# Pair and single-tile pipeline of a two-layer expert kernel: when z banks are filled, which engine copies, where sums are kept, when small DMAs leave

## The chip, the cores and the metric

The kernel runs on one core of one Trainium2 chip. The metric is device time in microseconds of one execution; the time before is the median of three runs. Engines are called by the names that the profile uses: PE (TensorE, matmuls; PEld its weight loads), DVE (VectorE), ACT (ScalarE), POOL (GpSimd) and SP (SyncE, which issues the DMAs here).

## The reference

An attention-like recurrence (4 x 768 tokens, 8 heads of 40) gives x of 3072 rows by 320 columns. A soft mixture of experts follows: 32 slots are averages of all rows, run through 8 small networks, and each row mixes the 32 results back. The last layer, on which nearly all of the change lies, is:

```python
P = np.exp(logits - logits.max())          # logits = x @ w_gate, 3072 x 8
for _ in range(8):                         # Sinkhorn: rows, then columns
    P /= P.sum(1, keepdims=True) + 1e-09
    P /= P.sum(0, keepdims=True) + 1e-09
    P *= N / E
for e in range(E):                         # E = 8, w1: 320 x 1024, w2: 1024 x 320
    ye = np.maximum(x @ w1[e], 0.0) @ w2[e]
    out += P[:, e:e + 1] * ye
```

## The kernel before, in words

The first 190 us are the recurrence and the soft mixture; the change doesn't touch them. Since x has rank 32 after that mixture, `x @ w1[e]` is computed as a product over 96 rows: three stacked f16 parts of the 32 routed rows times w1 (tile `Sst[e]`, made by `s1_p`, `s1_h`, `s1_l`, or for later experts by `s1_v`, `s1_w`) with three parts of the mixing weights (`cst`). Values are kept as a pair of f16 numbers, a high part and a low remainder, so that a product is three f16 matmuls.

The 3072 rows are 24 tiles of 128. Expert 0 is done for the first 20 tiles in blocks of 512 columns (functions `g1`, `g2`; a step `st` is one tile of `g2` and two z banks of `g1`). Beside these steps a list `EXTRA` sets further work of the following expert, and `sinkhorn` runs at every odd step: nine small DVE instructions, with one matmul for the sum over partitions. `g2` ends with a copy of its result y from PSUM to `acc`.

After that the work is a list of units, written in slots. A slot is a group of matmuls of about equal length:
- `Old`: one of the last four tiles of expert 0, 4 slots.
- `One` (letter c): one tile, 4 slots of 6 matmuls of 320 columns; it needs two z banks.
- `Two` (letter P): two tiles i and j at once by a Strassen-like scheme (Winograd's form), 7 slots of 12 matmuls of 160 columns instead of eight; it needs four z banks. Its left operands are the two column halves of the two tiles and sums of them; its right operands are quarters of w2 and sums of them (`sum_w`, `sum_h`, `sum_l`).

Experts 1 to 6 have the pattern `cPPcP` three times (87 slots, 24 tiles), expert 7 the pattern `LAST`. A z bank is one PSUM bank of 512 columns, filled by four matmuls (`z_`, L1540); there are three of them (`psz`), and five other PSUM banks (`psu`) hold x, z and y of the units. `produce(k)` fills z bank number k of a unit 11 - k slots ahead of it, and plans what reads the bank: ACT takes the relu as a high part (`hi_z`, L1546), DVE takes the relu plus or minus another tile (`relu_with`, L1549). The f32 results stand in one tile `tmr` of five parts, called r22, r21, s1_, s2, s3, and s4 uses the place of s1_. From these ACT makes f16 high parts (`cast`, L1621) and POOL the low remainders (`lo_s`, L1552). The first sum s1_ is made by POOL (L1630), or by DVE for every third pair. The f16 operands of a pair stand in `opr[buf % 2]`, those of a single tile in `chl[buf % 3]`.

`consume(k)` issues slot k's matmuls (L1574 for single tiles, L1671 for pairs) and plans the drains: `keep_m`, `drain_x`, `drain_z`, a copy of m into the z bank of the unit, and `drain_y`, which adds the pieces into `acc` with the weights `Ps`.

What sets the order: PE, ACT, DVE and POOL take their instructions in the order in which the program writes them (`manual_schedule`), each engine by itself, held only by data; a slot number is a place in that order and no time. SP's order is left to the scheduler. `when[c]` holds the functions planned for slot c, in the order in which they were entered; functions entered with `early` come first.

Further work per expert e, planned by slots from its start c, serves expert n = e + 1 or n + 1: `load_w2` and `load_m2w` (weights from DRAM), `amax` (largest value of w2), `pow2_w` and `pow2_s` (a power of two as scale, of w2 and of the s1 weights), `prep_a`, `prep_x`, `prep_y` (scaled high and low part of w2), the `sum_*` functions, and `s1_p` to `s1_w`. The scale needs a maximum over partitions. `pow2` with `later` takes it by two DMAs: a column of 128 numbers to DRAM (`col`, L1111), and from there broadcast to all partitions (`row`, L1112); the first DMA leaves at the first of two planned slots (`spread`), and at the second one DVE reads `row` (`pow2_b`, L1124).

Of the kernel before, what the change touches and what calls it, by code (L numbers as in the profile page):

```python
# [20 lines left out]
def mlstm_moe_kernel(  # L21
# [1291 lines left out]
    def g2(n, tt, k0=0, k1=KF):  # L1313
        e, tb = divmod(n, NB)
        hh, hl = hs[n]
        ts = slice(tt * P, (tt + 1) * P)
        if k0 == 0:
            y0[tt] = psy.tile([P, TB], F32, tag="y", name="y")[:, 0:DM]
        y = y0[tt]
        for kc in range(k0, k1):  # L1320
# [16 lines left out]
        if e == E - 1:  # L1337
            nc.sync.dma_start(out=out[i * P:(i + 1) * P, :], in_=a)
# [152 lines left out]
    def b_(e, n, a):  # L1491
# [41 lines left out]
    tmr = op_a.tile([P, 5, KH, P], F32, name="tmr")  # L1533
# [20 lines left out]
    class One:  # L1554
        slots, banks, tiles = 4, 2, 1
# [53 lines left out]
    class Two(One):  # L1609
        slots, banks, tiles = 7, 4, 2  # L1610

        def __init__(self, e, i, j, buf):
            self.e, self.i, self.j, self.buf = e, i, j, buf

        def produce(self, k, at):
            o = opr[self.buf % 2]
            r22, r21, s1_, s2, s3 = (tmr[:, m] for m in range(5))
            s4 = s1_
            z = z_(self.e, self.j if k < 2 else self.i, (1, 0, 0, 1)[k])
            hi, lo = (lambda m: o[:, m, 0]), (lambda m: o[:, m, 1])  # L1620
            cast = lambda m, x: nc.scalar.copy(out=hi(m), in_=x)  # L1621
            if k == 0:
                at(0, lambda: hi_z(r22, z))
            elif k == 1:
# [6 lines left out]
                at(1, lambda: lo_s(lo(2), r22, hi(2)))  # L1631
            elif k == 2:
                at(0, lambda: hi_z(hi(0), z))
                at(0, lambda: relu_with(s3, z, r21, ALU.subtract))
                at(0, lambda: relu_with(lo(0), z, hi(0), ALU.subtract))
                at(1, lambda: cast(3, s1_))
                at(1, lambda: relu_with(s2, z, s1_, ALU.subtract))
                at(2, lambda: lo_s(lo(3), s1_, hi(3)))
                at(2, lambda: cast(4, s3))
                at(3, lambda: lo_s(lo(4), s3, hi(4)))  # L1640
            else:
                at(0, lambda: hi_z(hi(1), z))
                at(1, lambda: relu_with(lo(1), z, hi(1), ALU.subtract))
                at(2, lambda: relu_with(s4, z, s2, ALU.add))
                at(2, lambda: cast(5, s2))
                at(3, lambda: lo_s(lo(5), s2, hi(5)))
                at(3, lambda: cast(6, s4))
                at(4, lambda: lo_s(lo(6), s4, hi(6)))

        def consume(self, k, at):  # L1650
# [26 lines left out]
            if k == 2:  # L1677
                at(1, self.keep_m, True)
# [20 lines left out]
        def drain_y(self):  # L1699
# [3 lines left out]
            self.plus(self.i, self.z[:, DH:3 * DH].rearrange("p (a d) -> p a d", a=2))  # L1703
            self.plus(self.j, self.z[:, 0:DH].unsqueeze(1).to_broadcast([P, 2, DH]))
# [39 lines left out]
    def plan(c, f, *a):  # L1744
        when.setdefault(c, []).append(lambda: f(*a))
# [36 lines left out]
    def steps(c, fs):  # L1782
        for d, f in zip((0, 16), fs):
            plan(c + d, f)

    for e in range(1, E - 1):
        c = base + (e - 1) * PER
        n = e + 1
        if n + 1 < E:
            plan(c + 2, load_w2, n + 1)  # L1790
            plan(c + 36, load_m2w, n + 1)
            plan(c + 35, pow2_w, n + 1, lambda *f, c=c: steps(c + 35, f))
        for kk in range(4):
            if n + 1 < E:
                plan(c + (19, 20, 30, 31)[kk], amax, n + 1, kk)
            plan(c + (5, 6, 16, 17)[kk], prep_a, n, kk)
            plan(c + (7, 8, 18, 19)[kk], prep_x, n, kk)
            plan(c + (9, 10, 20, 21)[kk], prep_y, n, kk)
        plan_sums(c, n, (38, 39, 49, 50), (41, 42, 52, 53), (67, 68, 78, 79))
# [3 lines left out]
        for k in range(3):  # L1803
            plan(c + 54 + k, s1_w, n, k)
# [12 lines left out]
    for u, c in zip(units, starts):  # L1817
        if c == base:
# [50 lines left out]
```

## Time and profile before

| | us |
|---|---|
| median of three runs | 892.33 |
| all three | 887.03, 892.33, 1458.84 |
| profiled execution | 891.81 |
| its span | 889.9 |
| PE busy in the span | 860.4 (97%) |
| DVE busy | 705.0 (79%) |
| POOL busy | 629.2 (71%) |
| ACT busy | 593.3 (67%) |

The span goes from the first to the last instruction of the profiled execution; the 1.9 us to its own time lie around it. Matmuls are pipelined, so a busy PE is not PE at its peak. The granted clock was 0.994 of full over the span.

### The profile page before, as it was taken

What the parts mean: (1) busy time and instruction counts of PE and PEld (TensorE: products, weight loads), DVE (VectorE), ACT (ScalarE), POOL (GpSimd) and SP (SyncE); (2) the same over time, 40 slices, a digit from 0 to 9 for tenths busy, and PEclk for the clock granted to TensorE, in tenths of its full rate; (3) what the DMA queues carried; (4) which work ended last, traced back from release to release, by engine and by line L of the source; (5) the groups of instructions that cost most, each with busy time, mean ns of one, the idle gap of its engine ahead of it and who ended that gap; (6) DMA issues with size and microseconds to landing.
All of it is one profiled execution on the core that took longest, in us unless ns stands there. A gap on an engine that the chain in (4) does not pass through costs nothing.

```text
span 889.9 us, 27440 instructions
## 1 busy us (share of the span) xinstructions
PE 860.4 (97%) x11284; PEld 739.1 (83%) x11284; DVE 705.0 (79%) x1570; ACT 593.3 (67%) x1210; POOL 629.2 (71%) x632
## 2 busy tenths in 40 slices
PE   7999997899989998999999999999999999999998
PEld 5888884346667996999899989989999998998997
DVE  7777876456897786788988888888897977787886
ACT  7656653353365986787778677867787687676763
POOL 5766661000054886998898889889988988898883
PEclk9999999999999998999999999999999999999999
DMA  8999999960101031102120311041102000000111
GB/s 170 187 190 184 195 244 319 330 192 1 60 1 60 2 60 23 60 2 62 22 62 2 63 20 60 3 67 46 32 1 67 17 2 2 11 11 23 47 54 60
DMA packets 136117, 67.09 MB, mean 75 GB/s; under 512 B 105049, under 2 KB 129753, under 8 KB 135993
## 3 DMA queue, kind: packets, MB, share of 16 engines
q1 hardware_dynamic: 135721, 64.86, 30.2%
q8 instruction: 88, 1.44, 0.7%
q14 instruction: 36, 0.29, 0.2%
q10 hardware_dynamic: 224, 0.30, 0.1%
q0 software_dynamic: 48, 0.20, 0.1%
HBM read 60.10 MB, written 5.02 MB: 73 GB/s over the span
## 4 chain that ended last, share of the span: by engine, by line
PE 74%; DMA 11%; DVE 10%; ACT 3%; issue 2%; POOL 1%; SPq 0%; ACTq 0%; DVEq 0%
PE y L1574 14%; PE z L1540 7%; DMA bigy<-in_moe_w_dram 3%; PE pss L432 2%; DMA col<-mxs 2%; PE oa L477 2%; PE ptk L383 2%; DVE tmr L1549 2%; PE y L1321 2%; PE y L1322 2%; PE y L1323 2%; DMA wa<-in_moe_w_dram 1%; PE pe L402 1%; PE ob L488 1%; DVE op L1549 1%
## 5 line engine op out<-in xcount | busy, mean ns | idle before, releaser
L1552 POOL TENSOR_TENSOR op<-tmr,op 128x512 f16<-128x512 f32 x320 | 365.1, 1165 | 49.9 <-ACT op L1621 47.6
L1671 PEld LDWEIGHTS <-op 128*128 128x128 f16 x5376 | 376.6, 98 | 4.6 <-issue 2.9
L1621 ACT CAST op<-tmr 128x512 f16<-128x512 f32 x320 | 195.4, 617 | 43.3 <-DVE tmr L1549 37.0
L1549 DVE SCALAR_TENSOR_TENSOR tmr<-z,tmr 128x512 f32<-128x512 f32 x213 | 144.8, 682 | 52.5 <-ACT op L1546 39.4
L1574 PE MATMUL y<-wx,ch 128*128 128x320 f16 x960 | 152.9, 302 | 0.0
L1540 PE MATMUL z<-cst,sst 96*128 96x128 f16 x1344 | 131.4, 220 | 6.6 <-DVE tmr L1549 5.3
L1574 PEld LDWEIGHTS <-ch 128*128 128x128 f16 x960 | 89.4, 98 | 28.6
L1540 PEld LDWEIGHTS <-sst 96*128 96x128 f16 x1344 | 97.4, 98 | 17.9 <-DVE tmr L1549 8.4
L1546 ACT ACTIVATE tmr<-z 128x512 f32<-128x512 f32 x128 | 73.4, 594 | 37.3 <-PE z L1540 36.3
L1549 DVE SCALAR_TENSOR_TENSOR op<-z,op 128x512 f16<-128x512 f32 x128 | 86.9, 679 | 0.0
L1546 ACT ACTIVATE op<-z 128x512 f16<-128x512 f32 x128 | 77.1, 602 | 0.0
L1630 POOL TENSOR_TENSOR tmr<-tmr 128x512 f32<-128x512 f32 x43 | 54.7, 1272 | 28.8 <-ACT tmr L1546 24.1
L1549 DVE SCALAR_TENSOR_TENSOR ch<-z,ch 128x512 f16<-128x512 f32 x80 | 53.6, 683 | 6.7 <-ACT ch L1546 6.7
L1303 ACT ACTIVATE hh<-z 128x512 f16<-128x512 f32 x48 | 26.6, 595 | 35.4 <-PE z L1300 35.1
L1323 PE MATMUL y<-wh,hl 128*128 128x320 f16 x160 | 48.3, 302 | 0.3 <-DVE hl L1304 0.3
L1321 PE MATMUL y<-wh,hh 128*128 128x320 f16 x160 | 48.5, 303 | 0.0
L1322 PE MATMUL y<-wl,hh 128*128 128x320 f16 x160 | 48.4, 303 | 0.0
L411 ACT ACTIVATE dd<-pe 128x512 f32<-128x512 f32 x48 | 29.2, 609 | 28.7 <-PE pe L402 28.4
L1546 ACT ACTIVATE ch<-z 128x512 f16<-128x512 f32 x80 | 45.4, 592 | 4.2 <-PE z L1540 4.2
L1116 POOL PARTITION_ALL_REDUCE mr<-mx x3 | 1.1, 383 | 63.1 <-DVE mx L1091 37.9
L1475 POOL TENSOR_TENSOR raw<-raw 128x640 f32<-128x640 f32 x28 | 43.4, 1549 | 1.2
L1481 POOL TENSOR_TENSOR wt<-raw,wt 128x640 f16<-128x640 f32 x28 | 38.8, 1407 | 7.6 <-ACT wt L1478 7.6
(1188 smaller groups left out, 1752.4 us busy)
## 6 DMA issues: line engine op xcount, KB each, us to landing
wa<-in_moe_w_dram SPq DMA_DIRECT2D x18, 512.0 KB
raw<-in_moe_w_dram SPq DMA_DIRECT2D x28, 320.0 KB
kq<-in_k_dram SPq DMA_DIRECT2D x24, 160.0 KB
kq<-in_q_dram SPq DMA_DIRECT2D x24, 160.0 KB
vz<-in_v_dram SPq DMA_DIRECT2D x24, 160.0 KB
xr<-in_o_gate_dram SPq DMA_DIRECT2D x24, 160.0 KB
wb<-in_moe_w_dram SPq DMA_DIRECT2D x6, 640.0 KB
out_dram<-acc SPq DMA_DIRECT2D x24, 160.0 KB
```

The lines of the kernel that those rows point to most:

```text
L1321: nc.tensor.matmul(y, hh[:, kc, ts], wh[e][:, kc, :], start=(kc == 0), stop=False)
L1322: nc.tensor.matmul(y, hh[:, kc, ts], wl[e][:, kc, :], start=False, stop=False)
L1323: nc.tensor.matmul(y, hl[:, kc, ts], wh[e][:, kc, :], start=False, stop=(kc == KF - 1))
L1475: nc.gpsimd.tensor_tensor(out=quarter(e, *o), in0=quarter(e, *a), in1=quarter(e, *b), op=op)
L1540: nc.tensor.matmul(z[:, k, :], Sst[e][:, kc * P:(kc + 1) * P], cst[:, i * P:(i + 1) * P], start=True, stop=True,)
L1546: nc.scalar.activation(out=o, in_=z, func=AF.Relu)
L1549: nc.vector.scalar_tensor_tensor(out=o, in0=z, scalar=0.0, in1=x, op0=ALU.max, op1=op)
L1552: nc.gpsimd.tensor_tensor(out=o, in0=x, in1=h, op=ALU.subtract)
L1574: nc.tensor.matmul(self.y, self.at(a, kc), b[self.e][:, kc, :], start=(kc == a == 0 and b is wh), stop=(kc == KF - 1 and a == 1),)
L1621: cast = lambda m, x: nc.scalar.copy(out=hi(m), in_=x)
L1630: at(0, lambda: nc.gpsimd.tensor_tensor(out=s1_, in0=r21, in1=r22, op=ALU.add))
L1671: nc.tensor.matmul(t[:, c * DH:(c + 1) * DH], o[:, m, a, kp, :], b[kp], start=(kp == a == 0 and b is bh), stop=(kp == KH - 1 and a == 1),)
```

## The change

- Expert 0's copies from PSUM, on DVE for 16 of its tiles so far, go to ACT.
- `EXTRA` is regrouped: two `s1_c` at step 8 and two at step 10 instead of one at each of 9 to 12, and the weight sums are spread differently; two `sum_l` go into the slots 6 and 8.
- `tmr` gets a second home: a pair uses `tmr[buf % 2]`, and s4 takes the place of r22 instead of s1_. `chl` has two homes instead of three.
- A pair's z banks are filled 11, 10, 8 and 6 slots ahead (before: 11, 10, 9, 8), and some casts and remainders are planned one slot later.
- Each planned function has a rank, and within a slot the lowest rank runs first: readers of z banks 0, casts and the other copies beside them 1, drains 2, planned weight work 3.
- The copy of m into a unit's z bank comes before `drain_z`; `drain_y` is spread over four slots (`sum_y`, two `plus`, the rest).
- The weight maxima, the weight load and the trip of `pow2_w` come later in an expert (67 instead of 35, the load 62 instead of 36), the reader of a trip 18 slots after its start instead of 16, `s1_w` two slots later.
- Which pair takes its first sum on DVE is written in the pattern (D): in experts 1 to 6 the second of three, as before; in expert 7 none. Expert 7 has eleven pairs and two single tiles (before: ten and four).

```diff
-        if n == 0:
+        if e == 0:
             nc.scalar.copy(out=a, in_=y)
-            return
-        if e == 0:
-            nc.vector.tensor_copy(a, y)
             return
...
-             8: [(prep_a, 0), (prep_s, 0)], 9: [(prep_a, 1), (prep_s, 1), (s1_c, 0)],
-             10: [(prep_a, 2), (prep_s, 2), (s1_c, 1), (b_, 2, 1)], 11: [(prep_a, 3), (prep_s, 3), (s1_c, 2)],
-             12: [(sum_w, 0), (sum_w, 1), (s1_c, 3)], 13: [(sum_w, 2), (sum_w, 3)],
-             14: [(sum_h, 0), (sum_h, 1)], 15: [(sum_h, 2), (sum_h, 3), (sum_l, 0), (sum_l, 1)],
-             16: [(sum_l, 2), (sum_l, 3)]}
+             8: [(prep_a, 0), (prep_s, 0), (s1_c, 0), (s1_c, 1)], 9: [(prep_a, 1), (prep_s, 1)],
+             10: [(s1_c, 2), (s1_c, 3), (prep_a, 2), (prep_s, 2), (b_, 2, 1)], 11: [(prep_a, 3), (prep_s, 3)],
+             12: [(sum_w, 0), (sum_w, 1)], 13: [(sum_h, 0)], 14: [(sum_h, 1), (sum_w, 2), (sum_w, 3)],
+             15: [(sum_h, 2), (sum_h, 3)], 16: [(sum_l, 0), (sum_l, 1)]}
...
-    tmr = op_a.tile([P, 5, KH, P], F32, name="tmr")
+    tmr = [op_a.tile([P, 5, KH, P], F32, name="tm0")]
...
-        slots, banks, tiles = 7, 4, 2
+        slots, banks, tiles, at_z = 7, 4, 2, (0,1,3,5)
...
-            r22, r21, s1_, s2, s3 = (tmr[:, m] for m in range(5))
-            s4 = s1_
+            r22, r21, s1_, s2, s3 = (tmr[self.buf % 2][:, m] for m in range(5))
+            s4 = r22
...
-                if self.buf % 3 == 1:
-                    at(0, lambda: relu_with(s1_, z, r22, ALU.add))
+                if self.add_v:
+                    at(0, lambda: relu_with(s1_, z, r22, ALU.add), 0)
                 else:
-                    at(0, lambda: nc.gpsimd.tensor_tensor(out=s1_, in0=r21, in1=r22, op=ALU.add))
+                    at(0, lambda: nc.gpsimd.tensor_tensor(out=s1_, in0=r21, in1=r22, op=ALU.add), 1)
...
-                at(2, lambda: cast(4, s3))
-                at(3, lambda: lo_s(lo(4), s3, hi(4)))
+                at(3, lambda: cast(4, s3), 1)
+                at(4, lambda: lo_s(lo(4), s3, hi(4)), 1)
...
-                at(3, lambda: cast(6, s4))
-                at(4, lambda: lo_s(lo(6), s4, hi(6)))
+                at(4, lambda: cast(6, s4), 1)
+                at(5, lambda: lo_s(lo(6), s4, hi(6)), 1)
...
-                at(1, self.drain_z)
-                at(2, lambda: nc.scalar.copy(out=self.z[:, DH:2 * DH], in_=self.m))
+                at(1, lambda: nc.scalar.copy(out=self.z[:, DH:2 * DH], in_=self.m), 1)
+                at(2, self.drain_z)
             elif k == 6:
-                at(1, self.drain_y)
+                at(1, self.sum_y)
+                at(2, lambda: self.plus(self.i, self.z[:, DH:3 * DH].rearrange("p (a d) -> p a d", a=2)))
+                at(3, lambda: self.plus(self.j, self.z[:, 0:DH].unsqueeze(1).to_broadcast([P, 2, DH])))
+                at(4, self.drain_y)
...
-    LAST = "PPcPPPcPPPcPPc"
+    KINDS = {1: "cPDcP" * 3, E - 1: "PPPPPcPPPPPPc"}
...
-            zat.setdefault(max(c - LEAD[type(u)] + k, 0), []).append((u, k))
+            zat.setdefault(max(c - LEAD + u.at_z[k], 0), []).append((u, k))
...
-        when.setdefault(c, []).append(lambda: f(*a))
+        when.setdefault(c, []).append((3, lambda: f(*a)))
+
+    def run(c):
+        fs = when.get(c, [])
+        while fs:
+            fs.pop(min(range(len(fs)), key=lambda k: fs[k][0]))[1]()
...
-        for d, f in zip((0, 16), fs):
+        for d, f in zip((0, 18), fs):
             plan(c + d, f)
+    plan(6, sum_l, 1, 2)
+    plan(8, sum_l, 1, 3)
+    PLANS = {
+        1: ((5, 6, 16, 17), (7, 8, 18, 19), (9, 10, 20, 21), (38, 39, 49, 50), (41, 42, 52, 53), (67, 68, 78, 79),
+            (19, 37, 48, 66, 67)),
...
+        at_a, at_x, at_y, *at_s, at_m = PLANS[1]
         if n + 1 < E:
             plan(c + 2, load_w2, n + 1)
-            plan(c + 36, load_m2w, n + 1)
-            plan(c + 35, pow2_w, n + 1, lambda *f, c=c: steps(c + 35, f))
+            plan(c + 62, load_m2w, n + 1)
+            plan(c + at_m[4], pow2_w, n + 1, lambda *f, c=c + at_m[4]: steps(c, f))
...
-                plan(c + (19, 20, 30, 31)[kk], amax, n + 1, kk)
+                plan(c + at_m[kk], amax, n + 1, kk)
...
-            plan(c + 54 + k, s1_w, n, k)
+            plan(c + 56 + k, s1_w, n, k)
...
-            chl.append(ot.tile([P, 2, KF, P], F16, name="ch2", bufs=1))
+            tmr.append(ot.tile([P, 5, KH, P], F32, name="tm1", bufs=1))
```

## Rows read from the trace of the kernel before

**Rows 1.** Short stretches: us, PE, PEld, DVE, ACT, POOL busy (x instructions), PEclk, DMA.
```profile
600.00:700.00 100.00, 99.86 (x1320) 91.79 (x1318) 85.67 (x184) 75.57 (x151) 89.24 (x75) 1.00 0.12 36
260.00:265.00 5.00, 2.69 (x16) 1.71 (x15) 4.84 (x8) 2.06 (x4) 4.22 (x3) 0.86 0.00 0
265.00:270.00 5.00, 5.00 (x30) 3.16 (x29) 4.27 (x13) 0.73 (x2) 0.00 (x0) 0.79 0.00 0
350.00:355.00 5.00, 4.70 (x25) 2.86 (x24) 4.85 (x12) 3.98 (x9) 3.89 (x5) 0.50 0.19 59
800.00:805.00 5.00, 4.33 (x64) 4.00 (x62) 1.70 (x4) 2.33 (x6) 5.00 (x5) 1.00 0.01 3
810.00:815.00 5.00, 4.12 (x62) 3.99 (x61) 4.00 (x11) 3.08 (x8) 1.27 (x2) 1.00 0.00 0
```

**Rows 2.** The chain in order of time: start us, us, what.
```profile
298.66 0.83 PE mx__4507 L1671 x12
...
320.60 1.00 PE pu L1017 x16
...
412.29 1.00 PE pu L1017 x16
...
582.24 1.00 PE pu L1017 x16
...
666.91 1.00 PE pu L1017 x16
...
883.30 3.27 PE y L1574 x24
```

**Rows 3.** PE's own waits: total us, times, longest us.
```profile
PE z L1540 <- DVE tmr L1549: 5.3, 4, 4.1
...
PE z L1300 <- DVE hl L1304: 2.3, 1, 2.3
...
PE z L1540 <- DVE ch L1549: 0.9, 1, 0.9
```

**Rows 4.** Timeline, trips of experts 1 and 6: start us, us, engine, line, what.
```profile
323.95 0.33 SPq L1111 DMA_DIRECT2D col<-iv  x1
...
332.40 2.29 SPq L1111 DMA_DIRECT2D col<-mxs  x1
...
347.12 0.28 DVE L1124 TENSOR_REDUCE iv<-row 128x1 f32<-128x128 f32 x1 [6.81 <-DMA row<-col]
...
756.96 0.34 SPq L1111 DMA_DIRECT2D col<-mxs  x1
```

**Rows 5.** The tile row: reader's ns min/median/max, first and last start.
```profile
L1124 DVE TENSOR_REDUCE iv<-row x11: 273/276/286, 339.0 to 770.0; 128x1 f32<-128x128 f32 x11
```

**Rows 6.** Costliest groups 196 to 282 us (DVE), timeline 196 to 250 us (ACT).
```profile
L1332 DVE COPY acc<-y 128x320 f32<-128x320 f32 x16 | 7.8, 487 | 4.5 <-PE y L1323 4.1
...
201.82 1.13 ACT L1329 COPY acc<-y 128x320 f32<-128x320 f32 x3
```

**Rows 7.** Timeline of DVE and POOL, a Sinkhorn multiply and the weight sums.
```profile
256.56 1.56 DVE L1407 TENSOR_TENSOR Pm<-Pm,ca 128x192 f32<-128x192 f32 x1
...
266.70 0.36 DVE L1407 TENSOR_TENSOR Pm<-Pm,ca 128x192 f32<-128x192 f32 x1
...
257.87 6.51 POOL L1475 TENSOR_TENSOR raw<-raw 128x640 f32<-128x640 f32 x4
```

**Rows 8.** Waits from 788 to 890 us.
```profile
POOL op L1552 <- ACT op L1621: 6.3, 6, 1.8
POOL tmr L1630 <- ACT tmr L1546: 4.3, 2, 2.1
DVE tmr L1549 <- POOL op L1552: 4.0, 3, 2.5
```

**Rows 9.** The page's costliest groups, POOL's part of a pair.
```profile
L1552 POOL TENSOR_TENSOR op<-tmr,op 128x512 f16<-128x512 f32 x320 | 365.1, 1165 | 49.9 <-ACT op L1621 47.6
...
L1630 POOL TENSOR_TENSOR tmr<-tmr 128x512 f32<-128x512 f32 x43 | 54.7, 1272 | 28.8 <-ACT tmr L1546 24.1
```

More of the change, by code (lines that the diff above doesn't have):

```diff
@@ L1554, in mlstm_moe_kernel @@
     class One:
-        slots, banks, tiles = 4, 2, 1
+        slots, banks, tiles, at_z = 4, 2, 1, (0, 1)
         def __init__(self, e, i, buf):
@@ new lines, in produce @@
+                at(0, lambda: relu_with(s3, z, r21, ALU.subtract), 0)
+                at(0, lambda: relu_with(lo(0), z, hi(0), ALU.subtract), 0)
+                at(1, lambda: cast(3, s1_), 1)
+                at(1, lambda: relu_with(s2, z, s1_, ALU.subtract), 0)
+                at(2, lambda: lo_s(lo(3), s1_, hi(3)), 1)
+                at(3, lambda: cast(4, s3), 1)
+                at(4, lambda: lo_s(lo(4), s3, hi(4)), 1)
+            else:
+                at(0, lambda: hi_z(hi(1), z), 0)
+                at(1, lambda: relu_with(lo(1), z, hi(1), ALU.subtract), 0)
+                at(2, lambda: relu_with(s4, z, s2, ALU.add), 0)
+                at(2, lambda: cast(5, s2), 1)
+                at(3, lambda: lo_s(lo(5), s2, hi(5)), 1)
+                at(4, lambda: cast(6, s4), 1)
+                at(5, lambda: lo_s(lo(6), s4, hi(6)), 1)
@@ L1720, in mlstm_moe_kernel @@
         i = 0
-        for c in "cPPcP" * 3 if e < E - 1 else LAST:
+        for c in KINDS.get(e, "cPDcP" * 3):
             if c == "c":
@@ L1725, in mlstm_moe_kernel @@
             else:
-                units.append(Two(e, i, i + 1, twos))
+                units.append(Two(e, i, i + 1, twos, c == "D"))
                 twos += 1
             i += units[-1].tiles
-    PER = sum(u.slots for u in units if u.e == 1)
-    LEAD = {One: 11, Two: 11}
+    LEAD = 11
     starts, c = [], 0
@@ L1782, in steps @@
     def steps(c, fs):
-        for d, f in zip((0, 16), fs):
+        for d, f in zip((0, 18), fs):
             plan(c + d, f)
+    plan(6, sum_l, 1, 2)
[3 more added lines that the diff above has]
+            (19, 37, 48, 66, 67)),
+        2: ((8, 15, 22, 34), (14, 16, 33, 35), (16, 17, 34, 36), (37, 47, 58, 59), (41, 51, 66, 73),
+            (60, 76, 77, 78), (30, 34, 59, 61, 62)),
+    }
     for e in range(1, E - 1):
-        c = base + (e - 1) * PER
+        c = starts[next(k for k, u in enumerate(units) if u.e == e)]
         n = e + 1
+        at_a, at_x, at_y, *at_s, at_m = PLANS[1]
         if n + 1 < E:
             plan(c + 2, load_w2, n + 1)
-            plan(c + 36, load_m2w, n + 1)
-            plan(c + 35, pow2_w, n + 1, lambda *f, c=c: steps(c + 35, f))
+            plan(c + 62, load_m2w, n + 1)
+            plan(c + at_m[4], pow2_w, n + 1, lambda *f, c=c + at_m[4]: steps(c, f))
         for kk in range(4):
             if n + 1 < E:
-                plan(c + (19, 20, 30, 31)[kk], amax, n + 1, kk)
[L1796 to L1799, printed above, removed]
+                plan(c + at_m[kk], amax, n + 1, kk)
+            plan(c + at_a[kk], prep_a, n, kk)
+            plan(c + at_x[kk], prep_x, n, kk)
+            plan(c + at_y[kk], prep_y, n, kk)
+        plan_sums(c, n, *at_s)
         plan(c + 33, s1_p, n)
@@ L1821, in mlstm_moe_kernel, with at @@
             opr.append(ot.tile([P, 7, 2, KH, P], F16, name="op1", bufs=1))
-            chl.append(ot.tile([P, 2, KF, P], F16, name="ch2", bufs=1))
+            tmr.append(ot.tile([P, 5, KH, P], F32, name="tm1", bufs=1))
         for k in range(u.slots):
             s_ = c + k
-            def at(d, f, early=False):
-                fs = when.setdefault(s_ + d, [])
-                fs.insert(0 if early else len(fs), f)
+            def at(d, f, p=2):
+                when.setdefault(s_ + d, []).append((p, f))
             for v, kk in zat.pop(s_, ()):
                 if type(v) is One and kk == 0:
-                    v.h = chl[v.buf % 3]
+                    v.h = chl[v.buf % 2]
                 v.produce(kk, at)
             u.consume(k, at)
-            while when.get(s_):
-                when[s_].pop(0)()
+            run(s_)
     for c in sorted(when):
-        while when[c]:
-            when[c].pop(0)()
+        run(c)
     man4.__exit__(None, None, None)
```

35 lines of the change are left out of this document (12 added, 23 removed).

## The prediction

> **What bounds the kernel now.** I read the busy table by stretches first. Between 600 and 700 us TensorE (PE) shows 99.86 of 100 us busy, at full clock, with 1320 matmuls, while VectorE (DVE), ScalarE (ACT) and GpSimd (POOL) show 76 to 89 [rows 1]. Busy time of pipelined matmuls proves little, so the chain of waits in order of time came next: it shows where PE's own pace sets the time. Twelve matmuls of 160 columns take 0.83 us, 69 ns each; one has 160 columns, 66.7 ns at the 2.4 GHz level. Twenty-four of 320 columns take 3.27 us, 136 ns each [rows 2]. So in the repeated part PE runs within 4% of its floor. The routed-weight product that occurs once per expert starts at 320.60, 412.29, 582.24 and 666.91 us [rows 2]: 91.69 us for the first period, 169.95 for the next two, 84.67 for the last. One period is 87 slots, 63 of a pair (0.83 us) and 24 of a single tile (3.27/4 = 0.82 us), so 52.3 + 19.6 = 71.9 us, and 12.8 us are left for 48 z banks and that product. Nothing in a settled period is to be won by reordering, except what hides in those 12.8 us.
>
> The gain must therefore come from the places where PE isn't at its pace. PE's own waits from 200 us on name three [rows 3], and the short stretches show what each costs [rows 1]:
> A, 260 to 270 us, expert 0: one wait of 2.3 us for DVE, then a granted clock of 0.86 and 0.79 of full, a mixture of the two levels. 0.21 x 5 = 1.05 us, and a part of 0.14 x 5 = 0.7 us: 3.7 us together.
> B, 345 to 355 us, expert 1: one wait of 4.1 us for DVE, then 5 us at clock 0.50, which is the 1.2 GHz level. 91.69 - 84.67 = 7.0 us by the two periods.
> C, 800 to 815 us, start of expert 7: PE idles 5.00 - 4.33 and 5.00 - 4.12, 1.55 us.
> PE's other waits on tmr are 5.3 - 4.1 = 1.2 us [rows 3], up to 0.67 of it in C; of the 0.5 us left I count 0.4 as late trips in other experts. All this is 12.7 us, 1.4% of the profiled time of 891.81 us.
>
> **The change part by part.**
>
> *DMA trips apart (B).* The maximum over partitions travels to DRAM and back by two small DMAs, col and row, and DVE then reads row. In expert 1 the weight trip leaves at 323.95 and its reader runs at 339.0; only after its row has been issued does the s1 trip leave, at 332.40, and DVE waits 6.81 us at the head of its queue, to 347.12 [rows 4, 5]. Behind that waiting instruction stand the reads of the z banks, and PE waits for a bank. A trip by itself lasts 770.0 - 756.96 = 13.0 us in expert 6, and 15.1 us with a weight load beside it (323.95 to 339.0) [rows 4, 5]. The change moves the weight trip from slot 35 to 67 and the load from 36 to 62, so that the s1 trip at slot 37 goes alone; and it puts the reader 18 slots after the start instead of 16. A slot is about 84.67/87 = 0.97 us, so 17.5 us are there for 13.0 (s1) and 15.1 us (weights behind the load). Both fit, so B goes whole: 7.0 us; bounds 0 (SP's order keeps the s1 trip behind something else) and 7.0. The 0.4 us of other experts goes by the same step. The weight trip is now wanted at slot 85, its first use is at slot 5 of the next expert; the load at 62 is wanted at slot 33 of the next, some 55 us on. Writing the new s1 weights two slots later leaves 18 slots to the first z product that reads them. Those three cost nothing.
>
> *Expert 0's copies on ACT, and its extra work regrouped (A).* Sixteen DVE copies of 487 ns leave (7.8 us in all), and ACT takes them at 1.13/3 = 0.38 us [rows 6]. Two of the s1 conversions leave the steps in which PE waited. But DVE's lateness there has a second source: a Sinkhorn multiply on Pm takes 1.56 us at 256.56 and 0.36 us at 266.70, and in between POOL runs its weight sums without a gap from 257.87 for 6.51 us [rows 7]. Both operands of the slow one lie in SBUF; it ends just behind a POOL instruction. POOL's order hardly changes: it runs ahead of PE and is not held by slots. So I take DVE as about 0.5 us earlier by the copy and 0.5 us by the conversion in that step, 1.0 of the 2.3 us, and half a microsecond of slow clock: 1.5 us. Bounds: 3.7 us won, and 2.3 us lost, if ACT with its added copies becomes as late as DVE was.
> The Trainium skill, "SBUF — State Buffer", section "SBUF: two separate sides", says that a DVE instruction with two SBUF inputs and a GpSimd instruction exclude each other on a shared port pair, for the whole instruction. The stretched multiply agrees with it. It speaks against this part: as the POOL sums stay beside the Sinkhorn pass, the rule alone would leave A as it is, and the sum would be 1.5 us worse; that is a rival below.
>
> *z banks at slots 0, 1, 3, 5; z reads first; sums drained in steps; copy of m before the sum v.* No instruction is added or removed in a settled expert; PE issues the same matmuls in another place. PE's pace hides it, so 0. If that cover is gone, it shows as PE waits on a z bank: the f16 pieces of a pair are now finished up to 3 slots later (the last at slot -1 instead of -4, wanted at slot 6), so 7 slots, 6.8 us, remain for POOL to be late, and the sum on POOL must be there 3 slots after it is queued. Bounds: 48 z banks of 512 columns need 10.2 us at 2.4 GHz and the product at least its 1.00 us, so of the 12.8 us at most 1.6 can be gaps; I let half of that, 0.8 us in each of five experts, be winnable (4 us); on the other side stands a loss like C's 1.55 us at each of two groups of weight sums in six experts (18.6 us). I take 0, since the nearest rows, three periods at PE's pace with POOL at 89% [rows 1, 2], are of the same work.
>
> *f32 sums in two homes.* tmr double takes away the wait of DVE for POOL's reading of the first home, 4.0 us in three waits after 788 us [rows 8], which is what C hangs on. C goes: 1.5 us, bounds 0 and 1.55.
>
> *Eleven pairs in expert 7.* Two single tiles, 2 x 3.27 = 6.54 us, become one pair, 84 x 69 ns = 5.81 us: 0.7 us won. But now all eleven sums fall to POOL, none to DVE. POOL per pair: 5 x 1.165 + 1.272 = 7.10 us [rows 9]; PE per pair: 5.81 us and four z banks of 12.8/48 = 0.27 us, 6.9 us at most. In the runs of five and six pairs POOL falls back by at least 0.2 us a pair, and starts with two weight sums still to do, at 6.51/4 = 1.63 us no more than 3.3 us [rows 7]. For the expert POOL needs 11 x 7.10 + 3.3 = 81.4 us; PE needs 11 x 5.81 + 2 x 3.27 + 48 x 0.27 = 83.4 us for 85 slots. From the first sum (10 slots ahead) to the last piece (5 slots before the end) there are 90 slots, 88 us: 7 us of air. Before, POOL idled there 6.3 + 4.3 us for ACT [rows 8]. If all 10.6 us stay, PE waits 3.7 us; if none, 0. I take 1.4 us lost, somewhat under the middle, as the two homes remove some of what made ACT late. Bounds for the expert with C: 2.2 us won, 3.7 - 0.7 = 3.0 us lost. Taken: -0.7 - 1.5 + 1.4 = -0.8.
>
> *The sum*, against the profiled execution's 891.81 us: -7.0 - 0.4 - 1.5 + 0 - 0.8 = -9.7, so 882.1. The median shown is 892.33, 0.5 us above the profiled one; I say 882.
>
> **The rivals.**
> *All gaps close:* A goes whole and the z filling gives its 4 us. 882.1 - 2.2 - 1.4 (POOL keeps up) = 878.5, and with the 4 us 874.5. For it: C and A hang on DVE's order. Against it: settled periods repeat to 84.67 us.
> *POOL's sums stretch the Sinkhorn pass as before, so A stays, and POOL sets expert 7's pace:* 882.1 + 1.5 + 3.7 - 1.4 = 885.9, and 887.4 if C's wait comes back there too. For it: the stretched multiply, and 81.4 us of POOL work in an expert of 83.4 [rows 7, 9]. Against it: the 7 us of air.
> *The trips change nothing:* SP issues in another order than the slots, as expert 1's already differs from the later ones, and DVE waits on the s1 trip again. 882.1 + 7.4 = 889.5. Against it: 17.5 us of room for 13.0.
> *Slower: the sum on POOL is late in every expert.* Place: DVE's head waits in the third z bank's last read for POOL's sum, queued 3 slots before, when weight sums (1.63 us each) stand in POOL's queue; reads come before drains, so nothing passes. Price: C's 1.55 us for each of 12 groups, 18.6 us: 882.1 + 18.6 = 901. It decides from 9.7/12 = 0.8 us per group on. Against it: POOL is idle for 11% of a settled stretch [rows 1].
>
> **How the numbers follow.** Forecast (879 to 885): 0.48. All gaps close: 0.13. A and expert 7 (885 to 889): 0.19. Trips: 0.07. Slower: 0.13. About 2% is what a measurement of this kernel can tell from no change, 17.8 us: below 874.5 only if every gap closes and the clock helps, 0.04; above 910 only the far end of the slower rival, 0.05; within, 0.91. The range leaves out half of the slower rival and the tip of the best one: 875.5 to 894.
>
> **What would show it.** Right: the product of expert 1 and that of expert 2 stand 85 us apart; no DVE wait on row; PE's wait near 260 us shorter; in expert 7 no wait of DVE for POOL's pieces, but POOL busy over 95% there. Wrong: periods over 85.5 us in experts 2 to 6, PE waits on tmr that repeat by expert, DVE waits on POOL's sum.

## The result, and the profile after

The changed kernel takes 878.43 us against 891.27 us of the kernel before in the same job, a ratio of 0.9879 (95% interval 0.985 to 0.9907). Each median counts one slow run (1458.84 us before, 1114.23 us after), and the ratio leaves both out. The changed kernel is faster, clear of the noise and by less than 2%. The profiled execution took 878.75 us with a span of 877.0; the one before had a span of 889.9. The forecast was 882.0, with 875.5 to 894.0 as its range. The time lies in the range, 0.6 us under the band of 879 to 885 that had the largest chance.

The short stretches (columns as in [rows 1]) show PE at its pace in the places that were read there:

```profile
600.00:700.00 100.00, 100.00 (x1337) 92.99 (x1336) 86.41 (x185) 75.47 (x154) 90.46 (x78) 1.00 0.12 36
255.00:260.00 5.00, 3.81 (x25) 2.00 (x24) 2.92 (x11) 4.88 (x10) 2.27 (x3) 1.00 0.00 0
260.00:265.00 5.00, 4.16 (x31) 2.87 (x30) 4.86 (x8) 2.43 (x6) 4.84 (x4) 1.00 0.00 0
345.00:350.00 5.00, 5.00 (x61) 4.39 (x60) 4.35 (x10) 5.00 (x12) 4.23 (x4) 1.00 0.20 62
800.00:805.00 5.00, 5.00 (x77) 4.92 (x75) 4.02 (x11) 3.55 (x8) 5.00 (x5) 1.00 0.01 2
```

At 345 and 800 us the gaps B and C of [rows 1] are gone: PE is busy for 5.00 of 5.00 us at full clock. Near 260 us a gap remains: 3.81 and 4.16 us busy, with 25 and 31 matmuls, but the granted clock stays at 1.00, where it had fallen to 0.86 and 0.79 before. PE's own waits from 200 us on, which answer to [rows 3]:

```profile
PE y L1321 <- ACT hh L1303: 0.9, 1, 0.9
PE z L1300 <- DVE hl L1304: 0.8, 1, 0.8
PE y L1323 <- DVE hl L1304: 0.3, 1, 0.3
PE z L1536 <- DVE tm L1545: 0.2, 1, 0.2
```

The waits on tmr (now tm) are 0.2 us in all instead of 5.3. Those near 260 us are 0.9 + 0.8 + 0.3 = 2.0 us in three pieces, where there was one of 2.3. The starts of the routed-weight product, from PE's timeline, answer to [rows 2]; those not shown are 488.10, 572.43 and 656.75:

```profile
229.63 1.07 PE L1017 MATMUL pu<-wa,soT 128*32 128x256 f32 x16
...
319.10 1.07 PE L1017 MATMUL pu<-wa,soT 128*32 128x256 f32 x16
...
403.78 1.07 PE L1017 MATMUL pu<-wa,soT 128*32 128x256 f32 x16
...
741.08 1.07 PE L1017 MATMUL pu<-wa,soT 128*32 128x256 f32 x16
```

These starts cut the span into stretches whose lengths repeat between most runs to 0.1 us, much closer than whole times. In the table "to first" ends at the product for expert 1. "A" is from there to the product for expert 2; it holds the rest of expert 0 and the first 33 slots of expert 1. "p1" to "p5" are the periods of experts 1 to 5, each from slot 33 of the expert to slot 33 of the next (product to product). "last" is the rest of the span: 54 slots of expert 6, and expert 7. Each number is a difference of two starts in that run's trace, in us. There is one trace for each run, and e2 to e10 are one execution each.

| run | to first | A | p1 | p2 | p3 | p4 | p5 | last | span |
|---|---|---|---|---|---|---|---|---|---|
| before | 228.92 | 91.61 | 91.69 | 84.93 | 85.02 | 84.68 | 84.66 | 138.41 | 889.9 |
| after | 229.63 | 89.48 | 84.67 | 84.32 | 84.33 | 84.32 | 84.33 | 135.95 | 877.0 |
| e1 trips together | 228.68 | 89.48 | 89.42 | 90.36 | 90.29 | 88.74 | 91.05 | 135.89 | 903.9 |
| e2 weight trip at 35 | 227.70 | 89.48 | 87.24 | 85.35 | 85.12 | 84.78 | 85.09 | 135.94 | 880.7 |
| e3 reader at 16 | 227.59 | 89.48 | 84.33 | 84.32 | 84.33 | 84.32 | 84.33 | 135.88 | 874.6 |
| e4 banks 0 1 2 3 | 225.50 | 89.86 | 84.34 | 84.34 | 84.34 | 84.34 | 84.34 | 138.01 | 875.1 |
| e5 and one home | 227.48 | 89.95 | 84.98 | 84.71 | 84.70 | 84.91 | 84.71 | 139.70 | 881.1 |
| e6 expert 7 as before | 227.20 | 89.47 | 84.66 | 84.32 | 84.33 | 84.32 | 84.33 | 136.10 | 874.7 |
| e7 copies on DVE | 231.16 | 90.90 | 84.68 | 84.32 | 84.33 | 84.32 | 84.33 | 135.96 | 880.0 |
| e8 old list | 231.36 | 87.46 | 84.65 | 84.32 | 84.33 | 84.32 | 84.33 | 135.95 | 876.7 |
| e9 no ranks | 230.89 | 89.47 | 84.33 | 84.32 | 84.33 | 84.32 | 84.33 | 135.80 | 877.8 |
| e10 sums on DVE in expert 7 | 227.88 | 89.48 | 84.68 | 84.32 | 84.33 | 84.32 | 84.33 | 135.39 | 874.7 |
| e11 before, trips apart | 232.42 | 88.48 | 85.36 | 84.92 | 84.91 | 85.14 | 84.92 | 139.02 | 885.2 |
| e12 combined | 229.61 | 87.49 | 84.36 | 84.32 | 85.00 | 84.50 | 84.33 | 135.38 | 875.0 |

The stretch to the first product lies between 225.5 and 232.4 us. The only code in it that any run changes is the engine of some copies in its last part, and from ACT's first copy of y to the product all 14 traces have 27.10 or 27.11 us; the spread lies ahead of that, in code that is the same in all. It alone moves whole times by 7 us, so the stretches decide, not the spans. From before to after: A -2.13, p1 -7.02, p2 and p3 -1.30, p4 and p5 -0.69, last -2.46, to first +0.71; together -12.9.

### The profile page after: what moved, and what is told of

The parts are those of the page before. It is cut to its first block, busy times and chain, and to the rows that moved or that the text cites. A ratio compares the mean times of both kernels' runs of the same rounds, so it can differ in the third digit from the quotient of the medians.

```text
span 877.0 us, 27362 instructions
## 1 busy us (share of the span) xinstructions
PE 855.6 (98%) x11320; PEld 739.4 (84%) x11320; DVE 696.0 (79%) x1558; ACT 597.9 (68%) x1233; POOL 636.4 (73%) x641
## 4 chain that ended last, share of the span: by engine, by line
PE 86%; DMA 5%; DVE 5%; ACT 2%; SPq 1%; issue 1%; POOL 0%; ACTq 0%; POOLq 0%; DVEq 0%
PE y L1570 15%; PE z L1536 9%; PE pss L432 3%; DMA bigy<-in_moe_w_dram 2%; PE oa L477 2%; PE ptk L383 2%; DMA wa<-in_moe_w_dram 2%; PE y L1321 1%; PE y L1322 1%; PE y L1323 1%; PE pe L402 1%; PE ob L488 1%; DVE hl L1304 1%; PE pu L1017 1%; DMA wb<-in_moe_w_dram 1%; PE z L1300 1%
## 5 line engine op out<-in xcount | busy, mean ns | idle before, releaser
L1548 POOL TENSOR_TENSOR op<-tm,op 128x512 f16<-128x512 f32 x325 | 370.6, 1164 | 55.9 <-ACT op L1617 50.1
L1667 PEld LDWEIGHTS <-op 128*128 128x128 f16 x5460 | 382.9, 98 | 1.5
L1617 ACT CAST op<-tm 128x512 f16<-128x512 f32 x325 | 197.2, 616 | 23.3 <-POOL tm L1626 21.3
L1545 DVE SCALAR_TENSOR_TENSOR tm<-z,tm 128x512 f32<-128x512 f32 x213 | 145.8, 684 | 69.1 <-ACT op L1542 63.7
L1570 PE MATMUL y<-wx,ch 128*128 128x320 f16 x912 | 139.6, 299 | 0.0
L1542 ACT ACTIVATE tm<-z 128x512 f32<-128x512 f32 x130 | 76.6, 599 | 49.9 <-PE z L1536 40.1
L1570 PEld LDWEIGHTS <-ch 128*128 128x128 f16 x912 | 84.9, 98 | 27.9
L1626 POOL TENSOR_TENSOR tm<-tm 128x512 f32<-128x512 f32 x47 | 59.9, 1274 | 6.0 <-ACT tm L1542 6.0
L1451 POOL TENSOR_TENSOR wx<-raw,wx 128x640 f16<-128x640 f32 x28 | 39.2, 1402 | 10.4 <-ACT sst L1237 7.5
L1304 DVE SCALAR_TENSOR_TENSOR hl<-z,hh 128x512 f16<-128x512 f32 x48 | 31.1, 685 | 18.8 <-ACT hh L1303 18.8
```

Source lines behind the costliest of these rows:

```text
L1542: nc.scalar.activation(out=o, in_=z, func=AF.Relu)
L1545: nc.vector.scalar_tensor_tensor(out=o, in0=z, scalar=0.0, in1=x, op0=ALU.max, op1=op)
L1548: nc.gpsimd.tensor_tensor(out=o, in0=x, in1=h, op=ALU.subtract)
L1570: nc.tensor.matmul(self.y, self.at(a, kc), b[self.e][:, kc, :], start=(kc == a == 0 and b is wh), stop=(kc == KF - 1 and a == 1),)
L1667: nc.tensor.matmul(t[:, c * DH:(c + 1) * DH], o[:, m, a, kp, :], b[kp], start=(kp == a == 0 and b is bh), stop=(kp == KH - 1 and a == 1),)
```

## The experiments

**Trips: together again (e1).**

```diff
-plan(c + 62, load_m2w, n + 1)
+plan(c + 36, load_m2w, n + 1)
-for d, f in zip((0, 18), fs):
+for d, f in zip((0, 16), fs):
-plan(c + 56 + k, s1_w, n, k)
+plan(c + 54 + k, s1_w, n, k)
```

The weight trip goes back from slot 67 to 35 and the four maxima ahead of it from 19, 37, 48, 66 to 19, 20, 30, 31.

> The changed kernel with the four edits of the DMA trips undone: weight trip at slot 35, load at 36, reader 16 slots after the start, s1 writes at 54; all else as changed. Theory 1, the two trips of expert 1 stand one behind the other in SP's queue, and DVE waits for the second: the period from expert 1's product to expert 2's goes from 84.7 back to about 91.7 us, a DVE wait on row of about 6.8 us, the later experts lose 0.3 each, time about 886. Rival, the ranks and the other fill places took the sting out of it: DVE still waits on row but PE doesn't, period under 86, time under 880.

907.06 us, ratio to before 1.0209 (1.0162 to 1.0256). It is the largest effect of all, and it goes past both theories: each of the five periods is 89 to 91 us, not only expert 1's. SP's timeline in expert 1 of this run, and DVE's two reads behind it:

```profile
322.94 0.33 SPq L1111 DMA_DIRECT2D col<-iv  x1
...
331.23 0.32 SPq L1112 DMA_DIRECT2D row<-col  x1
331.64 0.38 SPq L1111 DMA_DIRECT2D col<-mxs  x1
339.87 0.32 SPq L1112 DMA_DIRECT2D row<-col  x1
...
339.02 0.28 DVE L1124 TENSOR_REDUCE iv<-row 128x1 f32<-128x128 f32 x1
...
344.75 0.28 DVE L1124 TENSOR_REDUCE iv<-row 128x1 f32<-128x128 f32 x1 [4.87 <-DMA row<-col]
```

Col of the weight trip, its row, only then col and row of the s1 trip: SP sits in the wait of row for col, and the second trip starts 8.7 us after the first. In the kernel before, only expert 1 had this order [rows 4]; from expert 2 on both cols left ahead of both rows, as in its SP timeline of expert 2:

```profile
415.34 0.33 SPq L1111 DMA_DIRECT2D col<-iv  x1
...
417.86 0.33 SPq L1111 DMA_DIRECT2D col<-mxs  x1
422.97 2.63 SPq L1112 DMA_DIRECT2D row<-col  x2
```

In e1 all five experts have the serial order. DVE's waits of this run (total us, times, longest), and PE in the five microseconds around the second read:

```profile
DVE iv L1124 <- DMA row<-col: 26.3, 5, 6.2
```

```profile
343.00:348.00 5.00, 1.71 (x20) 1.22 (x17) 3.15 (x10) 2.36 (x6) 1.20 (x2) 1.00 0.17 11
```

PE does 20 matmuls in 5 us, busy for 1.71. In the changed kernel SP's order hangs on where the trips are planned; how much of it is lost hangs on the reader as well, as the next run shows.

**Only the weight trip back (e2).**

```diff
-            (19, 37, 48, 66, 67)),
+            (19, 20, 30, 31, 35)),
```

> The changed kernel with the weight maxima and the weight trip alone back (slots 19, 20, 30, 31 and 35), the load planned at 62 and the reader at 18. Theory 1, the trips' places in SP's queue decide: a second trip that lands some 30 us after the first leaves has 2 slots (1.9 us) more than before, so DVE waits about 5 us on row and the period of expert 1 is 88 to 90 us. Rival 2, the place of the load or the two slots more decide: no wait on row, period 84.7.

Expert 1's period is 87.24, the later ones 0.5 to 1.0 us over the changed kernel's. SP issues in the same serial order as in e1, but DVE waits little:

```profile
DVE iv L1124 <- DMA row<-col: 2.7, 4, 1.0
```

```profile
344.26 0.28 DVE L1124 TENSOR_REDUCE iv<-row 128x1 f32<-128x128 f32 x1 [0.38 <-DMA row<-col]
```

2.7 us instead of 26.3, so both theories are half right. Most of the loss is gone (e1's sum of five periods is 449.9 us, e2's 427.6, the changed kernel's 422.0), and the distance between the trips takes the rest. Three edits lie between e1 and e2: the reader, the load and the s1 write. The load starts to leave SP 0.70 us behind the product in both. The reader is what the traces show: the second row is read at almost the same time (344.75 and 344.26), but in e1 DVE has only the four small instructions of the first trip between the two reads, while in e2 five reads and drains of z banks and units stand between them and run meanwhile. The s1 write was not moved by itself.

**Only the reader back (e3).** `zip((0, 18), fs)` becomes `zip((0, 16), fs)`.

> The changed kernel with the reader of a trip 16 instead of 18 slots after its start. Theory 1: a trip alone takes 12 to 13 us from col to landing, 16 slots are 15.5 us, so nothing changes: all periods 84.3 to 84.7, time 878 to 879. Rival 3, the two slots more are what takes the wait away: DVE waits 1 to 2 us on row in several experts, periods up to 86.

876.29 us, no DVE wait on row, and all periods 84.3. With the trips apart the two slots are worth nothing (expert 1's period is even 84.33 instead of 84.67); either edit alone takes away most of the loss.

**Trips apart on the kernel before (e11).** The edits of e1 in the other direction, on the kernel before.

> The kernel before with the trip edits alone (weight maxima at 19, 37, 48, 66, weight trip at 67, load at 62, reader at 18, s1 writes at 56). Theory 1: expert 1's period falls from 91.7 to 84.7, the next two from 85.0 to 84.7, the settled ones stay at 84.67; time about 884, 7 to 8 us under before. Rival: without the ranks the maxima and readers come at worse moments, and periods stay over 85; time 886 to 890.

885.47 us against 889.26, ratio 0.997 (0.9946 to 0.9995). The time gains 3.8 us, half of what theory 1 said. By the stretches expert 1's period falls by 6.33 us, but the other four rise by 0.60 together and the last stretch by 0.61. Moved alone, the planned work costs in other places: PE now waits for DVE on z banks of single tiles (ch), 2.6 us in six waits instead of the one of 0.9 in [rows 3]:

```profile
PE z L1540 <- DVE ch L1549: 2.6, 6, 0.9
```

A was not to change, as the code of expert 0's steps is that of the kernel before, yet it is 88.48 instead of 91.61. The whole difference lies in those steps: from the product to the last matmul of `g2` it is 40.66 us here and 43.79 before. In this run, POOL's four low parts of w2 (`prep_y`) and DVE's Sinkhorn instructions beside them answer to [rows 7]:

```profile
256.10 5.59 POOL L1454 TENSOR_TENSOR wx<-raw,wx 128x640 f16<-128x640 f32 x4 [7.05 <-ACT wx L1149]
260.06 0.37 DVE L1407 TENSOR_TENSOR Pm<-Pm,ca 128x192 f32<-128x192 f32 x1
260.85 0.87 DVE L1393 TENSOR_SCALAR rw<-rw 128x24 f32<-128x24 f32 x1
```

```profile
PE z L1300 <- DVE hl L1304: 0.8, 1, 0.8
```

POOL's line in the kernel before:

```profile
252.32 5.59 POOL L1454 TENSOR_TENSOR wx<-raw,wx 128x640 f16<-128x640 f32 x4 [6.77 <-ACT wx L1149]
```

The multiply starts 27.64 us after the product for expert 1 here (260.06 - 232.42) and before (256.56 - 228.92). POOL's four instructions start 23.68 us after it here and 23.40 before. So here the multiply begins just ahead of the fourth (256.10 and three times 1.39 make 260.27) and takes 0.37 us; before, it began just behind the start of the fourth (256.5) and took 1.56. PE then waits 0.8 us here, 2.3 before, where the clock fell. The wait of 1.5 us more and the 1.05 + 0.7 us of slow clock there [rows 1] make 3.25 us, against 3.13 of the stretch. So a shift of 0.28 us on POOL goes with 3.1 us. The shift is POOL's idle time ahead of the four, 7.05 us here and 6.77 before; what sets that isn't shown.

**The four banks (e4).**

```diff
-        slots, banks, tiles, at_z = 7, 4, 2, (0,1,3,5)
+        slots, banks, tiles, at_z = 7, 4, 2, (0,1,2,3)
...
-                at(5, lambda: lo_s(lo(6), s4, hi(6)), 1)
+                at(4, lambda: lo_s(lo(6), s4, hi(6)), 1)
```

The other casts and remainders that the change planned a slot later go back by one as well.

> The changed kernel with a pair's z banks filled at 11, 10, 9 and 8 slots ahead again, and the casts and remainders at the slots of before; two homes, ranks and the rest as changed. Theory 1, the places of z banks are worth nothing while PE sets the pace: periods 84.3 to 84.4, last stretch from expert 6's product to the end 135.9. Rival, the spread is where the 0.34 us per settled expert came from: periods 84.6 to 85, last stretch 136 to 138, and PE waits for z banks return.

Settled periods 84.34, unchanged; last stretch 138.01, 2.06 us more. Theory 1 holds for experts 1 to 6, the rival for expert 7, where up to six pairs follow each other. PE has one wait for DVE there, 0.6 us near 794 us, which the changed kernel hasn't; where the other 1.5 us arise isn't shown.

```profile
PE z L1536 <- DVE tm L1545: 0.6, 1, 0.6
```

**And one home (e5).** On e4: `tmr[self.buf % 2]` becomes `tmr[0]`, `s4 = r22` becomes `s4 = s1_`.

> As the run with banks at 11, 10, 9, 8, and one home of the f32 sums as well, s4 in the place of s1_. Theory 1, the second home is what removed the wait at the start of expert 7: the last stretch goes up by about 1.5 us against that run, with DVE waits for POOL's remainders of 3 to 5 us there; settled periods up by 0 to 0.3. Rival, the ranks removed it: last stretch unchanged within 0.3 us.

The last stretch rises by 1.69 to 139.70, settled periods by 0.36 to 84.70, about the kernel before's 84.67. DVE's waits for POOL's remainders between 400 and 700 us, and PE at the start of expert 7:

```profile
DVE tm L1545 <- POOL op L1548: 9.2, 10, 1.2
```

```profile
790.00:795.00 5.00, 3.52 (x53) 3.28 (x51) 1.85 (x5) 1.97 (x6) 5.00 (x5) 1.00 0.00 0
```

9.2 us of waits that the changed kernel and e4 don't have, and a gap of 1.48 us in PE as in C. The second home is what settled experts gained from.

**Expert 7 as before (e6), and its sums on DVE (e10).** The first added line is e6, the second e10.

```diff
-    KINDS = {1: "cPDcP" * 3, E - 1: "PPPPPcPPPPPPc"}
+    KINDS = {1: "cPDcP" * 3, E - 1: "PDcPPDcPPDcPPc"}
+    KINDS = {1: "cPDcP" * 3, E - 1: "PDPPDcPPDPPDc"}
```

> The changed kernel with expert 7 as before: ten pairs, four single tiles, the same three sums on DVE. Theory 1, the eleventh pair is worth its PE time alone: last stretch 135.95 + 0.7 = 136.7. Rival, POOL's eleven sums cost something that the new pattern pays: last stretch 135 to 136.

> The changed kernel with four of expert 7's eleven first sums on DVE instead of POOL. Theory 1, POOL at its limit costs PE nothing, since its lateness stays inside the 7 slots: last stretch 135.9 within 0.2, POOL 5 us less busy there. Rival, POOL sets expert 7's pace, as one of the forecast's terms had it (1.4 us): last stretch 134 to 135.

e6: 136.10, only 0.15 more than the changed kernel; the rival's range misses it by little, theory 1 by 0.6. e10: 135.39, 0.56 less, between theory 1 and the rival. The two fit together: the eleventh pair gains 0.7 us (136.10 to 135.39) when DVE helps, and POOL's eleven sums give 0.56 of that back. From 780 to 875 us, first in the changed kernel, then in e10 (POOL is the last busy time):

```profile
780.00:875.00 95.00, 93.64 (x1312) 90.04 (x1309) 80.14 (x172) 64.03 (x135) 84.03 (x74) 1.00 0.13 42
```

```profile
780.00:875.00 95.00, 91.37 (x1286) 88.34 (x1283) 80.81 (x173) 62.60 (x133) 77.73 (x68) 0.99 0.13 44
```

POOL falls from 84.03 to 77.73 us busy. Neither run has a PE wait in that stretch by the list of waits, so it isn't shown where the 0.56 us sit.

**Expert 0: copies back on DVE (e7), old list (e8).**

```diff
-        if e == 0:
+        if n == 0:
             nc.scalar.copy(out=a, in_=y)
             return
+        if e == 0:
+            nc.vector.tensor_copy(a, y)
+            return
```

> The changed kernel with expert 0's sixteen copies back on DVE, its extra work regrouped as in the change. Theory 1, DVE is the late engine beside the Sinkhorn pass: the stretch from expert 1's product (near 229 us) to expert 2's goes from 89.48 to 90.5 to 92. Rival, ACT with its added copies is the late one now, as PE's wait of 0.9 us on hh shows: the stretch falls to 88 to 89.

Stretch A 90.90, 1.42 us more: theory 1. In e8 `EXTRA` is that of the kernel before, and the two `sum_l` at slots 6 and 8 go back into it:

> The changed kernel with the list of expert 0's extra work as before (one s1 conversion at each of the steps 9 to 12, the weight sums at 12 and 13), copies on ACT. Theory 1, what is lost near 260 us hangs on how Sinkhorn's DVE instructions fall beside POOL's sums, and regrouping gains nothing sure: stretch 88 to 90, with other instructions stretched. Rival, the regrouping is what gained: stretch 90.5 to 91.6.

Stretch A 87.46, 2.02 us less than the changed kernel and under theory 1's 88 to 90. So the regrouping loses, and the copies win. PE's waits from 228 to 300 us, e7 and then e8:

```profile
PE y L1321 <- ACT hh L1303: 1.4, 1, 1.4
PE z L1300 <- DVE hl L1304: 1.2, 1, 1.2
PE y L1323 <- DVE hl L1304: 0.3, 1, 0.3
```

```profile
PE z L1300 <- DVE hl L1304: 0.5, 1, 0.5
```

In sum PE waits 2.9 us in e7, 2.0 in the changed kernel and 0.5 in e8, so that these waits hold 0.9 of e7's 1.42 us and 1.5 of e8's 2.02. How the new list loses is in ACT's, DVE's and POOL's timeline of the changed kernel:

```profile
250.93 0.18 DVE L1390 TENSOR_SCALAR rw<-rw 128x24 f32<-128x24 f32 x1
...
254.11 0.47 ACT L1229 ACTIVATE sst<-pu,sc 32x256 f16<-32x256 f32 x1 [1.34 <-DVE sst L1233]
...
253.60 0.48 DVE L1233 SCALAR_TENSOR_TENSOR sst<-pu,sc,sst 32x256 f16<-32x256 f32 x1
...
257.71 1.29 DVE L1304 SCALAR_TENSOR_TENSOR hl<-z,hh 128x512 f16<-128x512 f32 x2 [1.85 <-ACT hh L1303]
...
260.12 1.13 DVE L1390 TENSOR_SCALAR rw<-rw 128x24 f32<-128x24 f32 x1
...
259.82 1.40 POOL L1451 TENSOR_TENSOR wx<-raw,wx 128x640 f16<-128x640 f32 x1 [1.61 <-ACT raw L1447]
```

With two s1 conversions in one step, ACT waits 1.34 us for DVE's part of the first before it begins the second, its relus come later, and DVE idles 1.85 us for them before its Sinkhorn pass, which then meets POOL's work: a 128 x 24 instruction takes 1.13 us instead of the 0.18 at 250.93. In e8 the pass is met as well, but DVE hasn't waited for ACT before it:

```profile
256.79 1.29 DVE L1304 SCALAR_TENSOR_TENSOR hl<-z,hh 128x512 f16<-128x512 f32 x2
...
259.24 1.09 DVE L1390 TENSOR_SCALAR rw<-rw 128x24 f32<-128x24 f32 x1
```

**Ranks (e9).** `fs.pop(min(...))` becomes `fs.pop(0)`, first entered, first run.

> The changed kernel without ranks: within a slot functions run in the order in which they were entered, so planned weight work comes first, as before. Theory 1, with two homes and trips apart the ranks are worth little: settled periods 84.3 to 84.5, last stretch within 0.5 of 135.95. Rival, the ranks keep z reads from waiting behind weight work of 0.8 to 1.6 us: periods 84.7 to 86, PE waits on z banks, last stretch 137 or more.

Periods 84.3, last stretch 135.80: the ranks are worth nothing here, theory 1.

**Combined (e12).** The changed kernel with e8's list, e10's pattern and e3's reader.

> The changed kernel with three of its parts taken back: expert 0's extra work listed as before, four of expert 7's first sums on DVE, the reader 16 slots after a trip's start. Theory, the parts add up as the single runs showed them: the stretch from expert 1's product to expert 2's 87.5 us (-2.0), expert 1's period 84.33 (-0.34), settled periods 84.33, last stretch 135.4 (-0.55): 2.9 us under the changed kernel, 875.5 us, ratio to before 0.982 to 0.986. Rival, the gain near 260 us hangs on how instructions happen to fall and doesn't come again: stretch 89 to 90, time 877.5.

876.79 us, ratio to before 0.9839 (0.9811 to 0.9866). A is 87.49 and the last stretch 135.38, both as the single runs had them. With the reader at 16 slots, though, two periods are 85.00 and 84.50: so close, a trip is sometimes late, and DVE waits on row, 0.9 us of it in expert 3:

```profile
DVE iv L1124 <- DMA row<-col: 2.2, 5, 0.9
```

The interval overlaps the changed kernel's (0.985 to 0.9907); that this version is better is likely by the stretches (1.99 less in A, 0.57 in the last one) and not shown by the times.

## Why the prediction was right, and where its steps were not

**B** was forecast at 7.0 us and measured 7.02 in expert 1's period. The mechanism held: one trip behind another in SP's queue, DVE at the head of the wait. By the runs the trips are worth somewhat less, 6.33 us in e11, and some 0.36 us of the 7.02 belong to the second home (e5). One step was wrong: "the load from 36 to 62, so that the s1 trip at slot 37 goes alone". SP's order isn't bound to slots, and in the changed kernel the load still leaves right behind the product, 7 us ahead of the s1 trip, whose reader then runs without a wait:

```profile
319.80 2.03 SPq L677 DMA_DIRECT2D wa<-in_moe_w_dram  x4
326.91 0.33 SPq L1111 DMA_DIRECT2D col<-mxs  x1
334.31 0.33 SPq L1112 DMA_DIRECT2D row<-col  x1
...
358.06 0.41 SPq L1111 DMA_DIRECT2D col<-iv  x1
...
343.62 0.28 DVE L1124 TENSOR_REDUCE iv<-row 128x1 f32<-128x128 f32 x1
```

What went apart is the weight trip (358.06 instead of 323.95). The 13.0 and 15.1 us of a trip were read from col's issue to a reader that didn't wait, so they are upper bounds; a trip alone takes about 12 us (last section). The price of the order was also not a constant: 3.8 us by e11 on the kernel before, and 907.06 against 878.43 us in the changed one, where SP's order made all five experts serial. The late trips of other experts were forecast at 0.4; of the 1.30 us in p2 and p3, about 0.7 belongs to the second home by e5.

**A** was forecast at 1.5 us and measured 2.13, but by other terms. "0.5 us earlier by the copy and 0.5 us by the conversion": the copies are worth 1.42 in e7, and the regrouping costs 2.02 in e8. These two don't sum to -2.13. But e11, with expert 0's code of the kernel before, has 88.48, and from there they nearly close: 88.48 - 1.42 + 2.02 = 89.08, against 89.48, which seven runs with the changed kernel's code of expert 0 and banks give within 0.01; 0.4 us stay open. So the 2.13 us are measured against an unlucky meeting of DVE and POOL in the profiled execution of before; how often that kernel meets it is open. Measured from e11, the two edits of expert 0 lose 1.0 us together, so that the term came out near its size is luck. What was won against that execution is the clock: PE's waits near 260 us went from 2.3 to 2.0 us only, but the 1.75 us that the slow clock cost there [rows 1] are gone, of which the forecast had counted half a microsecond.

The forecast's second source, the Sinkhorn pass stretched beside POOL's work, is there in all runs read, and the pair of before and e11 shows that the moment of the meeting decides. By the rule of the Trainium skill, "SBUF — State Buffer", section "SBUF: two separate sides", of a DVE instruction with two SBUF inputs and a GpSimd instruction that reads SBUF, whichever starts first holds a shared port pair for the whole instruction, and the other one waits. The trace agrees: the multiply took 0.37 us when it began just ahead of POOL's instruction, and 1.56 just behind its start. The rival drawn from this rule, that A stays as long as the pass is stretched, doesn't follow: in e8 PE's wait is 0.5 us with the pass still stretched.

**Settled experts** were forecast at 0, with 0.8 us per expert as a bound for smoother z filling. They gained 0.34, and the term was put to the wrong edit: the spread of the banks gives nothing there (e4), the second home 0.36 (e5), which the forecast priced in expert 7 alone. PE's idle time doesn't show it: DVE's ten waits for POOL in e5, 0.9 us on average, leave no wait in PE's list. The kernel before with its trips apart (e11) has 84.91 to 85.14 us there and e5 84.70 to 84.91, so some 0.2 us more may belong to edits that no run took back alone: the drains, the copy of m, the homes of `chl`.

**Expert 7 with C** was forecast at -0.8 and measured -2.46. The loss to POOL's pace, 1.4 us by the forecast, is 0.56 (e10), although POOL is as full as the forecast's sign had it, over 95% (79.19 of 80 us from 785 to 865 us). Its 7 us of air were 88 - 81.4 = 6.6, which makes the worst case 4.0 us and not 3.7. C's 1.5 us was right in size for the second home (1.69 by e5), but not all: the spread of the banks, forecast at 0, is worth 2.06 here. Eleven pairs in long runs need the two; with neither (e5), the last stretch is 139.70, longer than before. That is also why parts don't add up.

The **slower rival**, sums on POOL late in every expert, is refuted: POOL at 90% in a settled stretch leaves PE busy for 100.00 of 100 us. That **the trips change nothing** fell with expert 1's period. **All gaps close** (878.5) was nearest to the time, with B, C and the settled experts, but A's gap stayed. That the range held is owed to B first; of the 3.2 us by which the stretches went past the sum of -9.7, expert 7 and the settled experts hold the greater part.

## What to carry to other kernels

Look for two dependent round trips in one in-order DMA queue: what counts is which issue waits for which, and where the reader stands on its engine. Planned slots on the compute engines don't tell SP's order; read it from SP's timeline after each change. Where PE is at its pace, an added buffer can still shorten a settled period by a few tenths, and an edit that is worth nothing in a mixed pattern can be worth 2 us where equal units follow each other. Compare stretches between marks in the same instruction stream, since 7 us of unrelated spread can hide every part, and look at a stretch in more than one execution before an edit is credited with it.

## What the runs showed of the hardware that was not expected

A column of 128 numbers to DRAM and its broadcast back take long even with no other issue between them on SP's queue: in the changed kernel col to row's issue 7.4 us (326.91 to 334.31), and row 4.8 us to land in the median by the trace's table of DMA times, 12 us for 64 KB and less.

A PE wait of a few microseconds didn't always bring the clock down, and its length alone didn't decide it: waits of 0.9, 0.3 and 0.8 us near 260 us left the granted clock at 1.00, and a wait of 2.3 us there was followed by 0.79 in the kernel before. In e1 a wait of 3.4 us in expert 1 left it at 1.00 (343 to 348 us above), while one of 3.1 us in expert 2 was followed by 0.51:

```profile
435.00:440.00 5.00, 3.89 (x19) 2.51 (x20) 4.97 (x10) 3.48 (x7) 4.90 (x5) 0.51 0.08 26
```
